# A fused RWKV and conv-gated MoE kernel: one planned rank per part of a chunk, per converted piece and per block of the feed-forward, with traced lengths in the planner and all of w_in on one DMA queue

## The chip, the cores and the metric

The kernel runs on one core of a Trainium2 chip. A core has five engines, each with its own instruction stream that is executed in order: PE (matrix multiply; its weight loads are shown as PEld), DVE, ACT, POOL and SP, which here only issues DMAs. The metric is the device time of one execution in microseconds. Before the change the median of three runs is 386.65 us (386.19 to 386.65).

## The reference, cut to what matters

```
for t in range(S):                      # B=4, H=8 heads, S=768, D=48
    y[t]  = r[t] @ (state + u * k[t] x v[t])
    state = w[t] * state + k[t] x v[t]
x = y as (B, S, 384)
h = relu(x @ w_in)                      # w_in 384 x 1024
conv = 3-tap convolution of h along S, one set of taps per hidden column
out = (h * sigmoid(conv)) @ w_out       # w_out 1024 x 384
```

w_in, conv_w and w_out arrive as 64-bit floats, and the kernel turns them into pairs of 32-bit values on the chip.

## The kernel before, in words

**Work.** The recurrence is cut into 24 chunks of 128 time steps (six per batch, numbered 0 to 23 here). Part A of a chunk transposes w, k and r on PE (L541), runs two scans on DVE (L548, L555), scales keys and receptances (L553, L559), makes the diagonal on POOL (L583, L585, L589) and transposes the keys back (L597). Part B makes the scores (L662), puts them under the diagonal (L666), updates the state (L679, L683), and sums the carried part (L718; L692 and L695 in the first four chunks) and the part within the chunk (L728; L702 and L707) into y. Two copies (L710 and L711, from chunk 4 on L733 and L735) write y to `xT` as two parts. Chunk loads of w, k, r and v are four DMAs of 192 KB (L509).

The feed-forward works on eight blocks of 384 time steps, two per batch. Block 0 needs the `xT` of chunks 0 to 3, block 1 that of chunks 2 to 5. A block has eight hidden tiles: nine matmuls each (L755, three for each third of the 384 inputs), then a chain on ACT, DVE and POOL (L767 to L777) that frees the tile's PSUM bank at L774 and makes `gh`. Its three output tiles take eight steps of three matmuls each (L784), are copied by ACT (L814) into one of two `val` buffers and stored by SP (L815).

**Weights.** w_in comes in three column pieces (384, 384, 256), each by four DMAs, two for partitions 0 to 63 and two for 64 to 127; SP issues the first pair and ACT the second (L479, L483). A piece is converted only when all four have landed, in three parts; w_out has eight parts (L494). Each part takes four DVE instructions (L439, L444, L447, L450), two casts on ACT (L442, L459) and two POOL instructions (L453, L460).

**Order.** Nothing is issued in the order of the code. `Plan.op` records each step with an engine, a length from the table `LEN`, what it reads and writes, and a rank; `Plan.issue` plays the program through: whenever an engine is free it takes the ready step of lowest rank for which buffers are free. The order that comes out is the instruction stream. Ranks before are formulas: chunk n has 14n (its loads 10 earlier, part B 7 later), hidden tile f of a block a base plus 5f, converted pieces 5 apart. DMAs use eight semaphores in turn, so an issue waits until the DMA eight issues earlier has landed, whichever queue that one was on.

Of the kernel before, what the change touches and what calls it, by code (L numbers as in the profile page):

```python
# [24 lines left out]
CHUNK, LEAD, UNIT, DOWN, PIECE = 14.0, 0.0, 5.0, 1.6, 5.0  # L25
FIRST_IN, FIRST_OUT = -10.0, 60.0
AHEAD, GUARD = 10.0, 10.0
# [8 lines left out]
    tr=0.35, kback=0.35, scores=1.1, carried=0.9, state=0.42, y=0.95, mm3=0.53,  # L36
    scan=0.86, small=0.1, pad=0.07, kt=0.47, dg=0.47, cp=0.62, xlo=0.6, sd=0.22, s=0.27,
    stt=0.54, gate=0.47, wts=0.47, wstt=0.47,
    fill=0.25, kh=0.42, guard=0.72, sbd=0.34, xhi=0.49, relu=0.5, mul=0.49, sig=0.43, cast=0.42, out=0.37, exp=0.52,
    z=0.98, diag=1.07, lo=0.97,  # L40
    gather=1.6, carried_rows=1.4, y_rows=1.5,
    load=0.55, issue=0.45, spread=0.64,
)
TAIL = dict(PE=0.22, DVE=0.11, ACT=0.13, POOL=0.07, SP=2.2)
# [66 lines left out]
class Plan:  # L111
# [6 lines left out]
    def op(self, eng, us, f, r=(), w=(), holds=(), moves=0.0, port=False, rank=None):  # L118
        i, deps = len(self.ops), set()
        us = LEN[us] if isinstance(us, str) else us  # L120
# [18 lines left out]
        self.ops.append((eng, us, f, deps, bufs, moves, port, (self.rank if rank is None else rank) + i * 1e-6))  # L139

    def issue(self):
        n = len(self.ops)
        left = [len(o[3]) for o in self.ops]
        users = [[] for _ in range(n)]
        for i, o in enumerate(self.ops):
            for d in o[3]:
                users[d].append(i)
# [5 lines left out]
        for i in range(n):  # L153
            if not left[i]:
                ready[self.ops[i][0]].append((self.ops[i][7], i))
        events, order, t = [], [], 0.0
# [17 lines left out]
        while len(order) < n:  # L174
            for e in engines:
                if free[e] > t:
                    continue
                for k, (_, i) in enumerate(sorted(ready[e])):
                    if places(self.ops[i][4]):
                        break  # L180
                else:
                    continue
                ready[e].remove((self.ops[i][7], i))
                _, us, _, _, _, moves, port, _ = self.ops[i]
                at = t
                if e == "PE" and t < COLD:
                    us *= 1.4
# [5 lines left out]
                free[e] = at + us  # L193
                if moves:
# [5 lines left out]
            assert t < float("inf"), "no order found"  # L200
# [5 lines left out]
            for i in todo:  # L206
                if i < 0:
                    continue
                for b in self.ops[i][4]:
# [4 lines left out]
                for u in users[i]:  # L214
                    left[u] -= 1
                    if not left[u]:
                        ready[self.ops[u][0]].append((self.ops[u][7], u))
        self.order = order
        for _, i in order:
            for b in self.ops[i][4]:  # L220
                if b.kind.make and not b.made:
                    b.t, b.made = b.kind.make(), True
            self.ops[i][2]()
# [72 lines left out]
def rwkv_conv_moe_kernel(  # L296
# [177 lines left out]
    def win_pieces(f0, n, piece, after):  # L474
# [3 lines left out]
        for g, (eng, q) in enumerate((("SP", nc.sync), ("ACT", nc.scalar))):  # L478
            op(eng, "issue", lambda g=g, q=q: q.dma_start(  # L479
                out=raw.t[64 * g:64 * g + D, :, 0:2 * n],  # L480
                in_=w_in[0:6 * D, cs].rearrange("(m g i) c -> g i m c", m=KT, g=2)[g]), [after] if g else [], [(raw, 2 * g)], [raw],
                moves=3.5 * n / 1024)
# [3 lines left out]
                moves=1.2 * n / 1024)  # L486
        for m in range(KT):
            plan.rank = next(piece)
# [3 lines left out]
    def wout_pieces(t0, n, piece):  # L492
# [3 lines left out]
            [], [(raw, 0)], [raw], moves=0.95 * n)  # L496
        for t in range(n):
            plan.rank = next(piece)
# [5 lines left out]
    def loads(n):  # L504
# [3 lines left out]
        for nm, src in (("w", w), ("k", k), ("r", r), ("v", v)):  # L508
            op("SP", "load", lambda nm=nm, src=src: nc.sync.dma_start(  # L509
                out=st[nm].t[:, :, 0:D], in_=src[b, :, s, :].rearrange("h t d -> t h d")), [], [st[nm]], moves=1.15)  # L510
# [15 lines left out]
    def stage_a(n):  # L526
# [7 lines left out]
        def tr(src, t, cols):  # L534
# [4 lines left out]
            def f():  # L539
                for m in range(KT):  # L540
# [4 lines left out]
        wp, kp, rp = Buf(pa), Buf(pa), Buf(pa)  # L545
        op("DVE", "pad", lambda: nc.vector.memset(wp.t[:, 0:WID:SL], 0.0), [], [(wp, 1)], [wp])
# [3 lines left out]
            op0=ALU.mult, op1=ALU.add), [wp, (wp, 1)], [kr])  # L550
        tr(K_, kp, lambda m: kp.t[:, m * L:(m + 1) * L])
        op("DVE", "small", lambda: nc.vector.reciprocal(out=da.t[:, 0:WID - 1:SL], in_=kr.t[:, 0, 1:WID:SL]), [kr], [da])
        op("DVE", "kt", lambda: nc.vector.tensor_tensor(out=seg(kr.t[:, 0], 2), in0=thirds(kp.t), in1=seg(kr.t[:, 0], 2),  # L553
                                                        op=ALU.mult), [kp], [kr])
        op("DVE", "scan", lambda: nc.vector.tensor_tensor_scan(  # L555
# [4 lines left out]
                                                        op=ALU.mult), [rp], [(kr, 1)], [kr])  # L560
        if n < EARLY:
# [11 lines left out]
        else:  # L573
            for g in range(2):
                for m in range(KT):
# [3 lines left out]
                        [last], moves=0.05)  # L579
        if n == 0:  # L580
# [13 lines left out]

        def k_back():
# [310 lines left out]
```

## Time and profile before

| | |
|---|---|
| median of 3 runs | 386.65 us |
| span of the profiled execution | 387.1 us |
| PE busy | 350.6 us, 91% of the span |
| DVE, ACT, POOL busy | 281.8, 234.5, 174.6 us |
| DMA | 34.46 MB |

The profiled execution's own time is given as its span, first to last instruction; it is 0.45 us above the median. An engine's busy time is the union of its instructions. The rows in the last section but one give busy time by stretches, timelines of single engines with the idle time before an instruction and who ended it, and the page's slices.

### The profile page before, as it was taken

The numbers are of one execution on the slowest core, as the hardware profiler recorded it, in microseconds if no ns is written. First come the engines' busy times: TensorE is split into PE (matmuls) and PEld (weight loads), VectorE is DVE, ScalarE is ACT, GpSimd is POOL, SyncE is SP. The second block draws the span as 40 slices with busy tenths as digits, with TensorE's granted clock in tenths as the row PEclk, the third lists the DMA queues.
The fourth block names the chain that finished last, engine by engine and source line by source line (L and its number), as shares of the span: only waits on it lengthen the run. The fifth ranks groups of instructions, "written<-read, shape, count | busy, mean of one in ns | idle before, by whom it ended". The sixth has DMA issues, their size and how long they took to land.

```text
span 387.1 us, 7859 instructions
## 1 busy us (share of the span) xinstructions
PE 350.6 (91%) x2790; PEld 320.3 (83%) x2790; DVE 281.8 (73%) x575; ACT 234.5 (61%) x613; POOL 174.6 (45%) x199
## 2 busy tenths in 40 slices
PE   5545978798899999999999999999999999999992
PEld 2435856687688999998999999999999989999992
DVE  4357989999998688578776876688867774656520
ACT  4133766687776565389747663697664725766621
POOL 5265596865785444056443532454544310434320
PEclk9856999899999999999999999999999999999998
DMA  9999984422334354373323447244424130110001
GB/s 150 151 159 179 231 242 98 92 53 49 66 66 99 69 107 78 89 153 85 73 60 75 88 96 143 56 102 94 93 52 94 41 75 10 30 33 20 22 20 69
DMA packets 113571, 34.46 MB, mean 89 GB/s; under 512 B 103069, under 2 KB 110774, under 8 KB 113526
## 3 DMA queue, kind: packets, MB, share of 16 engines
q1 hardware_dynamic: 112852, 32.32, 40.9%
q10 hardware_dynamic: 674, 1.57, 2.0%
q8 instruction: 24, 0.39, 0.4%
q14 instruction: 21, 0.17, 0.1%
HBM read 25.19 MB, written 4.72 MB: 77 GB/s over the span
## 4 chain that ended last, share of the span: by engine, by line
PE 71%; DVE 11%; DMA 5%; issue 3%; SPq 3%; ACT 3%; POOL 2%; ACTq 0%; DVEq 0%; POOLq 0%
PE bank L784 25%; PE bank L755 23%; PE bank L662 6%; PE bank L728 4%; PE bank L541 4%; PE bank L718 4%; PE bank L679 2%; SPq L509 2%; DMA v<-in_v_dram 2%; DMA gh<-in_moe_w_in_dram 2%; PE bank L597 2%; DVE pm L666 1%; DVE a L771 1%; DMA r<-in_r_dram 1%; DVE e L444 1%
## 5 line engine op out<-in xcount | busy, mean ns | idle before, releaser
L755 PE MATMUL bank<-xT,wi 128*128 128x386 f32 x576 | 129.0, 349 | 2.2 <-ACT xT L710 1.7
L784 PE MATMUL bank<-wo,gh 128*128 128x384 f32 x576 | 127.2, 344 | 2.1 <-POOL wo L460 1.7
L777 POOL TENSOR_TENSOR gh<-g,gh 128x384 fp32r<-128x384 f32 x64 | 64.7, 1015 | 114.5 <-ACT gh L776 109.6
L755 PEld LDWEIGHTS bank<-xT,wi 128*128 128x128 f32 x576 | 101.6, 190 | 5.7 <-issue 2.0
L784 PEld LDWEIGHTS bank<-wo,gh 128*128 128x128 f32 x576 | 100.2, 188 | 4.3 <-POOL wo L460 2.0
L769 DVE SCALAR_TENSOR_TENSOR a<-bank,cw,a 128x384 f32<-128x384 f32 x64 | 38.6, 609 | 23.1 <-ACT a L768 22.9
L774 DVE TENSOR_TENSOR g<-bank,a 128x384 f32<-128x384 f32 x64 | 34.8, 549 | 19.0 <-ACT a L773 18.2
L773 ACT ACTIVATE a<-a 128x384 f32<-128x384 f32 x64 | 33.4, 522 | 23.9 <-DVE a L771 23.8
L767 ACT ACTIVATE bank<-bank 128x386 f32<-128x386 f32 x64 | 30.6, 478 | 25.4 <-PE bank L755 24.5
L589 POOL TENSOR_SCALAR_AFFINE_SELECT pm<-dg 128x1024 f32<-128x1024 f32 x24 | 26.2, 1092 | 41.5 <-PE bank L728 39.1
L776 ACT CAST gh<-g 128x384 fp32r<-128x384 f32 x64 | 32.5, 512 | 12.2 <-DVE g L774 12.1
L771 DVE SCALAR_TENSOR_TENSOR a<-bank,cw,a 128x384 f32<-128x384 f32 x64 | 38.8, 611 | 0.8
L666 DVE COPY_PREDICATED pm<-upper,bank 128x512 f32<-128x512 int32 x48 | 33.5, 725 | 5.5 <-PE bank L662 5.2
L768 ACT ACTIVATE a<-bank,cw 128x384 f32<-128x384 f32 x64 | 36.7, 581 | 0.5
L583 POOL TENSOR_TENSOR z<-r,k 128x384 f32<-128x384 f32 x24 | 24.4, 1016 | 12.2 <-DMA r<-in_r_dram 12.2
L548 DVE TENSOR_TENSOR_SCAN kr<-bank,one_end 128x387 f32<-128x387 f32 x24 | 22.9, 956 | 9.2 <-PE bank L541 9.1
L453 POOL TENSOR_TENSOR val<-val,e 128x384 f32<-128x384 f32 (+2 forms) x18 | 16.7, 927 | 19.1 <-DVE val L450 8.0
L585 POOL TENSOR_TENSOR z<-z,ubc 128x384 f32<-128x384 f32 x24 | 24.2, 1008 | 1.2
L662 PEld LDWEIGHTS bank<-kr 48*128 48x128 f32 x288 | 18.4, 188 | 7.0 <-issue 4.1
L662 PE MATMUL bank<-kr 48*128 48x128 f32 x288 | 23.2, 290 | 0.9 <-DVE val L450 0.9
L555 DVE TENSOR_TENSOR_SCAN kr<-bank,dA 128x387 f32<-128x387 f32 x24 | 22.9, 953 | 0.1
L541 PE MATMUL bank<-ident,k 128*128 128x128 f32 x72 | 13.0, 293 | 10.6 <-ACT k L535 10.6
(108 smaller groups left out, 523.7 us busy)
## 6 DMA issues: line engine op xcount, KB each, us to landing
w<-in_w_dram SPq DMA_DIRECT2D x24, 192.0 KB, 3.1
k<-in_k_dram SPq DMA_DIRECT2D x24, 192.0 KB, 3.5
r<-in_r_dram SPq DMA_DIRECT2D x24, 192.0 KB, 3.6
v<-in_v_dram SPq DMA_DIRECT2D x24, 192.0 KB, 3.1
out_dram<-val SPq DMA_DIRECT2D x24, 192.0 KB, 2.0
gh<-in_moe_w_out_dram SPq DMA_DIRECT2D x2, 1152.0 KB, 8.4
last<-kr SPq DMA_DIRECT2D x120, 16.2 KB, 1.8
xT<-xT SPq DMA_DIRECT2D x18, 64.0 KB, 2.4
```

The lines of the kernel that those rows point to most:

```text
L662: nc.tensor.matmul(sc[g].t[:, m * L:(m + 1) * L], lhsT=kt(m)[p], rhs=rt(m)[p], start=True, stop=True)
L666: op("DVE", "cp", lambda g=g: nc.vector.copy_predicated(out=pm.t[:, g], mask=upper.unsqueeze(1).to_broadcast([P, NP, L]), data=sc[g].t.rea ...
L755: nc.tensor.matmul(t.t[:, 0:xs.stop - xs.start], lhsT=wi[:, m, a, f * P:(f + 1) * P], rhs=xT[:, x0 + m, c, xs], start=(m == 0 and j == 0), ...
L767: ("ACT", "relu", lambda: nc.scalar.activation(out=h(0, width + 2), in_=h(0, width + 2), func=AF.Relu), [t], [t]),
L768: ("ACT", "mul", lambda: nc.scalar.mul(out=a(), in_=h(1), mul=cw[:, 1, f:f + 1]), [t, "cw"], [a1]),
L769: ("DVE", "stt", lambda: nc.vector.scalar_tensor_tensor(out=a(), in0=h(0), scalar=cw[:, 0, f:f + 1], in1=a(), op0=ALU.mult, op1=ALU.add), ...
L771: ("DVE", "stt", lambda: nc.vector.scalar_tensor_tensor(out=a(), in0=h(2), scalar=cw[:, 2, f:f + 1], in1=a(), op0=ALU.mult, op1=ALU.add), ...
L773: ("ACT", "sig", lambda: nc.scalar.activation(out=a(), in_=a(), func=AF.Sigmoid), [], [a1]),
L774: ("DVE", "gate", lambda: nc.vector.tensor_tensor(out=g.t[:, 0:width], in0=h(1), in1=a(), op=ALU.mult), [t, a1], [g]),
L776: ("ACT", "cast", lambda: nc.scalar.copy(out=part(0)[:, 0:width], in_=g.t[:, 0:width]), [g], [key]),
L777: ("POOL", "lo", lambda: nc.gpsimd.tensor_tensor(out=part(1)[:, 0:width], in0=g.t[:, 0:width], in1=part(0)[:, 0:width].bitcast(F32), op=AL ...
L784: nc.tensor.matmul(acc.t[:, 0:DM], lhsT=part(a)[:, tt * P:(tt + 1) * P], rhs=wo[:, f, c, :], start=(f == 0 and a + c == 0), stop=(f == FT ...
```

## The change

The eight constants that made the ranks are gone. A table `RANKS` gives a rank for every chunk and each of its thirteen parts, for each of the 17 converted pieces, the nine weight loads, conv_w, the 64 hidden tiles and the 24 output tiles. The lengths in `LEN` are replaced by others. The planner now adds a length to a PE step when the way the array is tiled changes from the step before. Both halves of w_in are issued by SP, and all weight loads are recorded right after chunk 0's part A. The planner's search was rewritten with heaps. What is computed does not change.

```diff
-CHUNK, LEAD, UNIT, DOWN, PIECE = 14.0, 0.0, 5.0, 1.6, 5.0
-FIRST_IN, FIRST_OUT = -10.0, 60.0
-AHEAD, GUARD = 10.0, 10.0
+DOWN = 1.6
...
+RANKS = dict(
+    load=[-61.9, -47.0, 30.3, -29.9, 60.4, 81.8, -3.6, 26.6, 138.8, 36.5, 47.1, 52.2, 177.2, 85.5, 116.3, 144.5,
+        214.8, 252.8, 48.3, 184.5, 256.7, 194.0, 153.2, 286.8],
...
+SWITCH = {(FULL, ROW): 0.17, (TRANS, ROW): 0.17, (COL, ROW): 0.17, (FULL, COL): 0.11, (TRANS, COL): 0.11,
+          (FULL, TRANS): 0.08, (COL, TRANS): 0.05}
...
+    def at(self, part, i, more=0.0):
+        self.rank = RANKS[part][i] + more
...
+                if e == "PE":
+                    us = us * (1.4 if t < COLD else 1.0) + SWITCH.get((mode, m), 0.0)
+                    mode = m
...
-        for g, (eng, q) in enumerate((("SP", nc.sync), ("ACT", nc.scalar))):
+        for g, (eng, q) in enumerate((("SP", nc.sync), ("SP", nc.sync))):
+            plan.at("rows", 2 * (f0 // HB) + g)
...
-            plan.rank = base + f * UNIT
+            plan.at("hidden", FT * bi + f)
...
-                plan.rank = base + FT * UNIT + (f * 3 + tt if last else tt * FT + f) * DOWN
+                plan.at("out", 3 * bi + tt, (3 * f if last else f) * DOWN)
```

On SP, at the start of the program, before (the letter is the input, the digit before the underscore its buffer; `gh` holds a raw piece of w_in):

```order
L509 DMA w0_120<-in_w_dram 128x8x48
L509 DMA k0_122<-in_k_dram 128x8x48
L509 DMA r0_124<-in_r_dram 128x8x48
L509 DMA v0_126<-in_v_dram 128x8x48
L479 DMA gh_176<-in_moe_w_in_dram 48x3x768
L483 DMA gh_176<-in_moe_w_in_dram 16x3x768
L509 DMA w1_121<-in_w_dram 128x8x48
L509 DMA k1_123<-in_k_dram 128x8x48
L509 DMA r1_125<-in_r_dram 128x8x48
L509 DMA v1_127<-in_v_dram 128x8x48
```

And now, where the first piece of w_in comes with all four DMAs behind eight chunk loads:

```order
L592 DMA v0_126<-in_v_dram 128x8x48
L592 DMA w1_121<-in_w_dram 128x8x48
L592 DMA k1_123<-in_k_dram 128x8x48
L592 DMA r1_125<-in_r_dram 128x8x48
L592 DMA v1_127<-in_v_dram 128x8x48
L562 DMA gh_185<-in_moe_w_in_dram 48x3x768
L566 DMA gh_185<-in_moe_w_in_dram 16x3x768
L562 DMA gh_185<-in_moe_w_in_dram 48x3x768
L566 DMA gh_185<-in_moe_w_in_dram 16x3x768
L592 DMA w0_120<-in_w_dram 128x8x48
L592 DMA w1_121<-in_w_dram 128x8x48
```

Chunk 1's loads moved ahead of the first piece, and the loads of chunks 2 and 3 follow it in pairs.

On ACT, around the fill of chunk 1's k (`k1`), before:

```order
L535 COPY w1_121<-w1_121 128x2x3x16
L605 ACTIVATE junk_75,flags_112<-w1_121,guard_hi_110 128x384
L442 ACTIVATE bank2_66<-bank2_66,ebias_118 128x384
L459 CAST wi_116<-val0_72 128x384
L479 DMA gh_179<-in_moe_w_in_dram 48x3x768
L535 COPY k1_123<-k1_123 128x2x3x16
L535 COPY r1_125<-r1_125 128x2x3x16
```

and now:

```order
L618 COPY w1_121<-w1_121 128x2x3x16
L698 ACTIVATE junk_75,flags_112<-w1_121,guard_hi_110 128x384
L698 ACTIVATE junk_75,flags_112<-w1_121,guard_lo_108 128x384
L618 COPY k1_123<-k1_123 128x2x3x16
L618 COPY r1_125<-r1_125 128x2x3x16
```

The DMA issue that stood ahead of `k1` on ACT is gone, and no conversion stands between them.

On PE, at the first hidden tile (`xT` times `wi`) and the scores of chunk 4 (from `kr1`), before:

```order
L755 MATMUL bank4_68<-xT_113,wi_116 128x386 x9
L662 MATMUL bank6_70<-kr1_134 128x128
...
L728 MATMUL bank6_70<-pm0_154,v1_127 48x128 x8
L755 MATMUL bank2_66<-xT_113,wi_116 128x386 x3
```

and now:

```order
L855 MATMUL bank1_65<-xT_113,wi_116 128x386 x3
L855 MATMUL bank3_67<-xT_113,wi_116 128x386 x3
L855 MATMUL bank1_65<-xT_113,wi_116 128x386 x3
L855 MATMUL bank3_67<-xT_113,wi_116 128x386 x3
L855 MATMUL bank1_65<-xT_113,wi_116 128x386 x3
L855 MATMUL bank3_67<-xT_113,wi_116 128x386 x3
L855 MATMUL bank4_68<-xT_113,wi_116 128x386 x3
L757 MATMUL bank6_70<-kr1_134 128x128
```

Two hidden tiles and a third of the next stand ahead of chunk 4's scores, where one stood.

## Rows read from the trace of the kernel before

**Rows 1.** The page: busy time and share of each engine, and the span in 40 slices (tenths of busy time).

```profile
PE 350.6 (91%) x2790; PEld 320.3 (83%) x2790; DVE 281.8 (73%) x575; ACT 234.5 (61%) x613; POOL 174.6 (45%) x199
PE   5545978798899999999999999999999999999992
```

**Rows 2.** Busy time by stretches: us, then busy us of each engine with its instructions, the granted clock, the DMA engines' share, GB/s.

```profile
0.00:57.00 57.00, 36.17 (x293) 28.80 (x293) 36.94 (x88) 26.02 (x82) 31.96 (x57) 0.82 1.01 181
57.00:70.00 13.00, 8.64 (x96) 7.08 (x94) 12.99 (x29) 9.02 (x28) 8.20 (x10) 1.00 0.45 111
70.00:114.00 44.00, 40.02 (x301) 34.60 (x302) 43.23 (x89) 33.17 (x85) 31.36 (x33) 0.96 0.34 69
114.00:380.00 266.00, 265.63 (x2106) 249.78 (x2105) 188.46 (x370) 165.82 (x418) 103.08 (x102) 1.00 0.33 71
```

**Rows 3.** The timeline of ACT at the fills of k for chunks 1 and 2: start, length, what, and in brackets the idle time before it and who ended it. ACTq is a DMA issue.

```profile
20.64 0.51 ACT L459 CAST wi<-val 128x384 fp32r<-128x384 f32 x1
25.63 0.32 ACTq L479 DMA_DIRECT2D gh<-in_moe_w_in_dram  x1
25.99 0.27 ACT L535 COPY k<-k 128x96 f32<-128x96 f32 x1 [4.83 <-DMA gh<-in_moe_w_in_dram]
...
34.70 0.27 ACT L535 COPY k<-k 128x96 f32<-128x96 f32 x1 [3.07 <-DMA v<-in_v_dram]
```

**Rows 4.** The timeline of PE at the same two places.

```profile
26.31 0.90 PE L541 MATMUL bank<-ident,k 128*128 128x128 f32 x3 [5.43 <-ACT k L535]
...
35.02 0.90 PE L541 MATMUL bank<-ident,k 128*128 128x128 f32 x3 [3.40 <-ACT k L535]
```

**Rows 5.** Who DVE waited for in the first 57 us: total us, times, longest.

```profile
DVE bank L439 <- DMA gh<-in_moe_w_in_dram: 5.6, 1, 5.6
DVE e L444 <- ACT bank L442: 5.2, 2, 4.3
DVE kr L548 <- PE bank L541: 2.9, 1, 2.9
```

**Rows 6.** Busy time of two early stretches of 10 us, columns as in rows 2.

```profile
10.00:20.00 10.00, 5.45 (x50) 4.82 (x48) 3.75 (x9) 2.41 (x9) 2.64 (x4) 0.79 1.06 152
...
30.00:40.00 10.00, 5.67 (x32) 4.96 (x30) 7.64 (x15) 4.54 (x16) 6.07 (x6) 0.66 1.15 178
```

**Rows 7.** The timeline of DVE: the first conversion, and a stretch without idle time.

```profile
17.39 0.56 DVE L439 TENSOR_SCALAR bank<-gh 128x384 int32<-128x384 int32 x1 [5.57 <-DMA gh<-in_moe_w_in_dram]
...
89.10 0.61 DVE L771 SCALAR_TENSOR_TENSOR a<-bank,cw,a 128x384 f32<-128x384 f32 x1
89.62 0.73 DVE L666 COPY_PREDICATED pm<-upper,bank 128x512 f32<-128x512 int32 x1
90.24 0.54 DVE L450 SCALAR_TENSOR_TENSOR val<-gh,bank 128x384 f32<-128x384 uint32 x1
90.70 0.55 DVE L774 TENSOR_TENSOR g<-bank,a 128x384 f32<-128x384 f32 x1
```

**Rows 8.** The timeline of PE, at the first hidden tile and at the eighth output step.

```profile
69.94 0.45 PE L755 MATMUL bank<-xT,wi 128*128 128x386 f32 x1 [1.67 <-ACT xT L710]
70.69 2.94 PE L755 MATMUL bank<-xT,wi 128*128 128x386 f32 x8 [0.30 <-DVE xT L711]
...
90.92 1.08 PE L728 MATMUL bank<-pm,v 128*48 128x128 f32 x16
91.93 0.80 PE L755 MATMUL bank<-xT,wi 128*128 128x386 f32 x3
...
112.38 1.22 PE L784 MATMUL bank<-wo,gh 128*128 128x384 f32 x6
```

**Rows 9.** The timeline of PE in the stretch without idle time.

```profile
203.30 0.49 PE L597 MATMUL bank<-ident,kr 128*128 128x128 f32 x3
203.54 0.78 PE L755 MATMUL bank<-xT,wi 128*128 128x386 f32 x3
204.16 0.69 PE L784 MATMUL bank<-wo,gh 128*128 128x384 f32 x3
204.69 0.69 PE L755 MATMUL bank<-xT,wi 128*128 128x386 f32 x3
...
210.59 0.94 PE L662 MATMUL bank<-kr 48*128 48x128 f32 x12
...
211.68 0.67 PE L679 MATMUL bank<-v,kh 128*64 128x48 f32 x16
212.28 0.91 PE L718 MATMUL bank<-kr,sbd 112*112 112x128 f32 x6
...
213.25 0.49 PE L541 MATMUL bank<-ident,w 128*128 128x128 f32 x3
213.58 0.49 PE L541 MATMUL bank<-ident,k 128*128 128x128 f32 x3
```

**Rows 10.** The timeline of ACT at the end of the program.

```profile
378.99 1.00 ACT L814 COPY val<-bank 128x384 f32<-128x384 f32 x2 [6.71 <-PE bank L784]
381.45 0.48 ACT L814 COPY val<-bank 128x384 f32<-128x384 f32 x1 [1.47 <-DMA out_dram<-val]
```

**Rows 11.** The page's DMA issues: KB each and us from issue to landing.

```profile
last<-kr SPq DMA_DIRECT2D x120, 16.2 KB, 1.8
```

**Rows 12.** The timeline of SP, where it issues the six small DMAs of a chunk (`last`).

```profile
66.28 3.94 SPq L576 DMA_DIRECT2D last<-kr  x6
```

More of the change, by code (lines that the diff above doesn't have):

```diff
@@ L35 @@
 LEN = dict(
[L36 to L40, printed above, removed]
+    tr=0.3, kback=0.3, scores=0.93, carried=0.8, state=0.6, y=1.0, mm3=0.53,
+    scan=0.875, small=0.1, pad=0.07, kt=0.465, dg=0.44, cp=0.62, xlo=0.6, sd=0.3, s=0.265,
+    stt=0.527, gate=0.465, wts=0.461, wstt=0.461,
+    fill=0.172, kh=0.335, guard=0.61, sbd=0.364, xhi=0.483, relu=0.41, mul=0.475, sig=0.426, cast=0.418, out=0.375,
+    exp=0.48, z=0.97, diag=1.06, lo=0.966,
     gather=1.6, carried_rows=1.4, y_rows=1.5,
@@ L44 @@
+FULL, TRANS, ROW, COL = range(4)
+MODE = dict(tr=TRANS, kback=TRANS, gather=TRANS, carried=TRANS, carried_rows=TRANS, scores=ROW,
+            state=COL, y=COL, y_rows=COL)
+SWITCH = {(FULL, ROW): 0.17, (TRANS, ROW): 0.17, (COL, ROW): 0.17, (FULL, COL): 0.11, (TRANS, COL): 0.11,
+          (FULL, TRANS): 0.08, (COL, TRANS): 0.05}
 TAIL = dict(PE=0.22, DVE=0.11, ACT=0.13, POOL=0.07, SP=2.2)
@@ L138, in op, with reset, run @@
                     t.kind.wanted += 1
[L139 to L147, printed above, removed]
+        self.ops.append((eng, us, f, deps, bufs, moves, port, self.rank + i * 1e-6, mode))
+    def reset(self):
+        kinds, stores = {}, {}
+        for o in self.ops:
+            for x in o[4]:
+                kinds[id(x.kind)] = x.kind
+        for k in kinds.values():
+            k.held = k.served = k.wanted = 0
+            stores[id(k.places)] = k
+        for k in stores.values():
+            if not hasattr(k, "all"):
+                k.all = list(k.places)
+            k.places[:] = k.all
+        seen = set()
+        for o in self.ops:
+            for x in o[4]:
+                if id(x) not in seen:
+                    seen.add(id(x))
+                    x.t, x.uses, x.turn = None, 0, x.kind.wanted
+                    x.kind.wanted += 1
+                x.uses += 1
+    def run(self, ranks):
+        self.reset()
+        ops, n = self.ops, len(self.ops)
+        left = [len(o[3]) for o in ops]
         engines = ("PE", "DVE", "ACT", "POOL", "SP")
@@ L154, in issue @@
             if not left[i]:
-                ready[self.ops[i][0]].append((self.ops[i][7], i))
-        events, order, t = [], [], 0.0
+                heapq.heappush(ready[ops[i][0]], (ranks[i], i))
+        events, order, t, end, mode = [], [], 0.0, 0.0, FULL
         def places(bufs):
@@ L193, in issue @@
                 free[e] = at + us
+                end = max(end, free[e])
                 if moves:
@@ L213, in issue @@
                         b.kind.places.append(b.t)
-                for u in users[i]:
+                for u in self.users[i]:
                     left[u] -= 1
                     if not left[u]:
-                        ready[self.ops[u][0]].append((self.ops[u][7], u))
+                        heapq.heappush(ready[ops[u][0]], (ranks[u], u))
+        return order, end
+    def issue(self):
+        ops, n = self.ops, len(self.ops)
+        self.users = [[] for _ in range(n)]
+        for i, o in enumerate(ops):
+            for d in o[3]:
+                self.users[d].append(i)
+        ranks = [o[7] for o in ops]
+        order, end = self.run(ranks)
         self.order = order
         for _, i in order:
-            for b in self.ops[i][4]:
+            for b in ops[i][4]:
                 if b.kind.make and not b.made:
                     b.t, b.made = b.kind.make(), True
-            self.ops[i][2]()
+            ops[i][2]()
 def general(ctx, tc, r, k, v, w, u, out, const, ident, x, moe_block):
```

126 lines of the change are left out of this document (87 added, 39 removed), and 4 rows, old and new, of the table hidden.

## The prediction

> **What bounds the kernel now.** I read the page first. PE is busy for 91% of the span, DVE for 73%; the slices show that PE's missing share lies at the start and in the last slice, where everything between is 9 [rows 1]. Then I cut the span where the character changes [rows 2]. From 114 to 380 us PE is busy 265.6 of 266 us: nothing but less work for PE shortens that. From 70 to 114 us it is DVE that is full (43.2 of 44), and PE loses 4.0 us in small waits. From 57 to 70 us DVE is full as well (13.0 of 13), PE has 8.6. From 0 to 57 us neither is: PE has 36.2, DVE 36.9, and the DMA engines are busy throughout (share 1.01). So PE's idle time is 20.8 + 4.4 + 4.0 + 0.4 = 29.6 us, and behind it a tail of 7 us. Anything that a new order gains has to come out of these 29.6, by bringing DVE through its early work sooner, or out of the tail.
>
> Who made DVE wait early: the first conversion for w_in's first piece (5.6 us), an instruction behind ACT (4.3), and the start (2.9) [rows 5]. The 4.3 and two waits of PE have one origin. ACT had finished a cast at 21.15 and then stood before a DMA issue until 25.63, because that issue waits for an earlier DMA to land; the fill of k for chunk 1 was queued behind it. The same happened before the fill at 34.70, with 3.07 us [rows 3]. PE, which needs the filled k, waited 5.43 and 3.40 us there [rows 4].
>
> **The change, step by step.** *Lengths, SWITCH, heaps, RANKS* cost nothing themselves: they act in the planner, and what counts is the order.
>
> *w_in by SP.* Six issues leave ACT, at 0.32 us each [rows 3] some 1.9 us, and with them the two waits of 4.8 and 3.1 us. SP gets six issues more. It has nothing else to do, and its DMA engines were the limit anyway: 152 to 178 GB/s in the early stretches at a share of 1.06 to 1.15 [rows 6]. The bytes are the same, so I take no DMA time gained or lost; from outside, half of ACT's waits could come back as later landings (4 us), or the shared engines gain a little (1 us). The Trainium skill, "DMA: Bandwidth & Descriptors", section "Issuing engines are not separate DMA queues", says that DMAs started by several engines share the same 16 DMA engines, and that starting them on several saves only the sequencer's issue time. By that rule alone the two halves on one queue would return the 1.9 us of issue time to ACT, and the forecast would be some 5 us higher; the trace shows more than issue time, the 7.9 us for which ACT was held ahead of its fills.
>
> *When data arrives.* The first piece of w_in now stands behind eight loads: 8 x 192 + 1152 KB = 2.75 MB. Before, 2.16 MB had gone when the piece was there at 17.3 us [rows 7]; 0.59 MB more at 0.152 MB/us is 3.9 us: 21.2 us. The loads of chunks 2 and 3 (1.57 MB at 0.16) are then in at 31 us. The second piece, with half of the third and conv_w mixed in (1.6 MB at 0.178), is complete at 40.
>
> *DVE until the first hidden tile.* Both orders need the xT of chunks 0 to 3. Before, the fourth copy released PE at 70.69 us [rows 8]; DVE had been busy for 49.9 of the first 70 [rows 2], so it had idled for 20. Counted along DVE, exactly twelve instructions fewer now stand ahead of it, all of conversions, 0.46 us apart (90.24 to 90.70) [rows 7]: 5.5 us less, 45 us of work. Idle time now: the start 3.9 us (to the first scan, as before); chunks 0 and 1 keep DVE fed to about 17.5 (11.5 us of work to the first xT copy, some waits), then up to 4 us for the piece at 21.2; from there work runs to 40, where the second piece arrives, say 1 us; 3 to 4 us for small waits on PE and ACT. Sum 12.5 us; bounds 8 (the piece costs nothing) and 20 (all idle time returns elsewhere). The fourth xT copy is then done at 57.5, and PE's first hidden tile starts at 58.5 instead of 69.94 [rows 8]. PE's own work ahead of it, 44.8 us by then [rows 2], fits.
>
> *From there to block 1.* In the new order PE does, from the first hidden tile of block 0 to that of block 1, 24 thirds and 20 output steps at 0.53 us, three scores at 1.09, two states at 0.60, two carried at 0.97, seven transposes at 0.33, two back at 0.24 [rows 9], three y at 1.01 [rows 8]: 23.3 + 12.2 = 35.5. A step after another tiling takes 0.62 in place of 0.53 (203.54 to 204.16) [rows 9]; 15 such returns add 1.4: 36.9. DVE in the same stretch, up to the xT copy of chunk 5: 27 conversion instructions at 0.46, 24 of hidden tiles at 0.52 (89.10 to 89.62) [rows 7], and 25 of attention: 12.4 + 12.6 + 11.3 = 36.3. The two are level, so I charge the waits that PE has when DVE is full: 4.0 per 44 us [rows 2], here 3.5. Block 1 starts at 58.5 + 36.9 + 3.5 = 98.9 us.
>
> *The same work before.* At 112.38 us [rows 8] PE had done 33 thirds and 7 output steps, and of attention the same but for one transpose group and one back more. Four steps less those two are 1.55 us: before was there at 113.9. So 15.0 us are won at this point.
>
> *Given back.* DVE stays near full until the conversions are through, at about 135 us; at the same rate 3.5 us go there. I count 228 changes of tiling along PE against 220 before, at 0.09 us: 0.7 us.
>
> *The tail.* Before, the last block's three output tiles end together. ACT copies two at 378.99 and the third waits 1.47 us, to 381.45, for a store to release its buffer [rows 10]. Now one of the three ends eight steps (4.2 us) early, and the last finds a free buffer: 1.3 us won.
>
> Sum: 387.1 - 15.0 + 3.5 + 0.7 - 1.3 = 375.0 us of span. The profiled execution's span stands 0.45 us above the median; the forecast of the median is 374.6 us.
>
> **Rivals.**
> 1. *The early idle time stays.* DVE waits for w_in as long as before in sum, 20 us: each piece needs all four DMAs, and with 64 partitions of it behind loads and behind another piece's halves the last quarter can be late. For it: the DMA share above 1 [rows 6]. Against it: the waits of rows 3 are tied to an issue that is gone. Then the first tile starts at 66 instead of 58.5; 7.5 us less gain: 382.1.
> 2. *A late wait takes it back.* The new order packs chunks 20 to 23 tightly ahead of the last two blocks: from the y of chunk 19 to that of chunk 23 PE finds only eleven output steps between the chunks. Each chunk needs six small DMAs through SP (3.94 us to issue) [rows 12], the last landing 1.8 us later [rows 11], into one of two buffers that is free only after the carried part two chunks back. I count 6.4 us of PE work between release and need for chunk 21, against 5.7 to 6 for the DMAs: room of half a us. If other issues on SP stand ahead of them, each of the four chunks becomes a chain: DMAs 5.7, scores 1.1, masking two times 0.62 (89.62 to 90.24) [rows 7], y 1.0, about 9 us where PE has about 5 of work, 16 us in all: 390.6, slower. It decides when the DMAs start 3 us late in each round; for it, SP's strict order; against it, that PE lost 0.4 us in 266 with the same DMAs in looser order [rows 2].
> 3. *The order changes nothing that counts*: gains early, but PE, short of ready hidden tiles later, loses as much: 386. PE's full stretch speaks against it.
> 4. *More is won*: DVE idles for only 8 us early and the waits of 3.5 twice do not occur: 375 - 4.5 - 5 = 365.5 at most.
>
> **How the numbers follow.** The forecast (370 to 380) has 0.55, rival 1 (380 to 385.8) 0.20, rival 2 0.13, rival 3 0.05, rival 4 (below 370) 0.07. A measurement of this kernel can tell about 0.2% from no change, that is 385.9 to 387.4. Faster by more than that: 0.55 + 0.20 + 0.07 = 0.82. Within it: 0.05. Slower: 0.13. The range from 368 to 386 leaves out rival 2, the lower part of rival 4 and half of rival 3: just under 0.2.
>
> **What would show it.** In the changed profile: no DMA issue on ACT before a fill of k, and PE's waits of 5.4 and 3.4 us gone; the first hidden tile at 56 to 61 us; DVE idle 11 to 14 us before it; PE through block 1's first hidden tile by 99; at most 4 us of idle PE from there to 135 and 1 us after; the last copy on ACT without a wait for a store. A first hidden tile after 64 would show rival 1, idle PE above 5 us after 250 rival 2, and idle time spread over 135 to 370 would show rival 3.

## The result and the profile after

The changed kernel takes 373.65 us (median of 4 runs, 373.06 to 375.82) against 386.65: a ratio of 0.967, 95% interval 0.964 to 0.970. The forecast was 374.6.

The traced execution of the changed kernel has a span of 371.4 us. First the page, which answers to [rows 1], with the slices of the granted clock:

```profile
PE 347.4 (94%) x2790; PEld 317.2 (85%) x2790; DVE 281.7 (76%) x575; ACT 233.9 (63%) x613; POOL 174.5 (47%) x199
PE   7967776999999999999999999999999999999992
PEclk9999996999999999999999999999999999999998
```

And its stretches, the columns as in [rows 2]:

```profile
0.00:57.00 57.00, 43.96 (x402) 35.10 (x402) 47.93 (x113) 33.74 (x108) 38.48 (x64) 1.00 0.94 193
57.00:70.00 13.00, 10.91 (x72) 9.71 (x74) 12.14 (x26) 10.91 (x28) 9.95 (x10) 0.74 0.34 93
70.00:114.00 44.00, 42.67 (x335) 38.25 (x332) 40.64 (x86) 30.73 (x81) 27.80 (x28) 1.00 0.42 90
114.00:364.00 250.00, 249.61 (x1985) 234.03 (x1983) 180.83 (x352) 157.92 (x396) 98.27 (x97) 1.00 0.32 71
```

Most of what changed is in the first row. DVE does 47.9 us of work in the first 57 us instead of 36.9, PE 44.0 instead of 36.2. PE's idle time in the four stretches was 20.8, 4.4, 4.0 and 0.4 us before; it is 13.0, 2.1, 1.3 and 0.4 now. Behind 114 us PE is full in both kernels. Every span here splits into three parts: PE's idle time up to its last instruction, its busy time, and the tail behind it. Before: 29.5 + 350.6 + 7.0 = 387.1. After: 16.9 + 347.4 + 7.1 = 371.4. So 12.6 us of idle time went, and 3.2 us of busy time, though PE executes the same 2790 instructions. The busy time goes with the clock: before, the granted clock was at half (1.2 instead of 2.4 GHz) from 15.9 to 29.5, from 32.9 to 39.8 and from 70.5 to 73.9 us; after, only from 58.8 to 65.7. PE was busy for 13.1 us of the first three stretches and 5.0 of the last; if half of that is the price of the clock (an estimate), it is 6.5 against 2.5 us. The page's slices of the granted clock before, to set beside those above:

```profile
PEclk9856999899999999999999999999999999999998
```

The fills of k for chunks 1 and 2 on ACT, where [rows 3] have waits of 4.83 and 3.07 us behind a DMA issue:

```profile
8.78 0.19 ACT L698 ACTIVATION_READ_ACCUMULATOR junk<-w,guard_lo 128x1 f32 x1
8.87 0.25 ACT L618 COPY k<-k 128x96 f32<-128x96 f32 x1
...
21.03 0.54 ACT L524 ACTIVATE bank<-bank,ebias 128x384 int32<-128x384 int32 x1
21.49 0.26 ACT L618 COPY k<-k 128x96 f32<-128x96 f32 x1
```

No wait and no DMA issue is left there, and chunk 1's k is filled at 8.87 us instead of 25.99. PE's timeline, to be read beside [rows 4], [rows 8] and [rows 9]: the transposes of k for chunks 1 and 2, the first hidden tile, what follows it, the first step of block 1, and the only wait behind 114 us:

```profile
11.39 0.49 PE L624 MATMUL bank<-ident,k 128*128 128x128 f32 x3
...
21.80 0.55 PE L624 MATMUL bank<-ident,k 128*128 128x128 f32 x3 [0.88 <-ACT k L618]
...
51.44 0.44 PE L855 MATMUL bank<-xT,wi 128*128 128x386 f32 x1 [0.43 <-ACT xT L809]
...
57.24 0.82 PE L757 MATMUL bank<-kr 48*128 48x128 f32 x9 [0.98 <-DVE e L526]
...
62.06 4.18 PE L855 MATMUL bank<-xT,wi 128*128 128x386 f32 x13 [1.85 <-DVE val L532]
...
97.76 0.78 PE L855 MATMUL bank<-xT,wi 128*128 128x386 f32 x3
...
281.42 0.55 PE L689 MATMUL bank<-ident,kr 128*128 128x128 f32 x3 [0.39 <-DVE kr L640]
```

Of the waits of 5.43 and 3.40 us the first is gone and the second is 0.88. The first hidden tile starts at 51.44 instead of 69.94, block 1 at 97.76. DVE's first conversion, which stood idle for 5.6 us before [rows 5]:

```profile
18.21 0.56 DVE L521 TENSOR_SCALAR bank<-gh 128x384 int32<-128x384 int32 x1 [1.05 <-DMA gh<-in_moe_w_in_dram]
```

The piece of w_in itself comes no earlier (18.21 against 17.39). What changed is how much other work stands ahead of it on DVE.

### The profile page after: what moved, and what is told of

It is laid out like the page before. It is cut to its first block, busy times and chain, and to the rows that moved or that the text cites. A ratio compares the mean times of both kernels' runs of the same rounds, so it can differ in the third digit from the quotient of the medians.

```text
span 371.4 us, 7867 instructions
## 1 busy us (share of the span) xinstructions
PE 347.4 (94%) x2790; PEld 317.2 (85%) x2790; DVE 281.7 (76%) x575; ACT 233.9 (63%) x613; POOL 174.5 (47%) x199
## 4 chain that ended last, share of the span: by engine, by line
PE 71%; DVE 15%; DMA 3%; ACT 3%; issue 3%; SPq 3%; POOL 1%; DVEq 0%; ACTq 0%
PE bank L855 26%; PE bank L884 24%; PE bank L827 5%; PE bank L757 5%; PE bank L817 4%; PE bank L624 4%; DMA gh<-in_moe_w_in_dram 2%; PE bank L776 2%; SPq L592 2%; DVE kr L632 2%; PE bank L689 1%; DVE val L532 1%; DVE pm L762 1%; DVE kr L643 1%; DVE a L869 1%
## 5 line engine op out<-in xcount | busy, mean ns | idle before, releaser
L855 PE MATMUL bank<-xT,wi 128*128 128x386 f32 x576 | 123.3, 350 | 2.4 <-DVE val L532 1.8
L884 PE MATMUL bank<-wo,gh 128*128 128x384 f32 x576 | 122.8, 344 | 1.2 <-POOL wo L542 1.0
L884 PEld LDWEIGHTS bank<-wo,gh 128*128 128x128 f32 x576 | 99.2, 188 | 4.1 <-POOL wo L542 1.7
L869 DVE SCALAR_TENSOR_TENSOR a<-bank,cw,a 128x384 f32<-128x384 f32 x64 | 38.2, 612 | 26.3 <-ACT a L868 26.0
L873 ACT ACTIVATE a<-a 128x384 f32<-128x384 f32 x64 | 33.4, 524 | 20.7 <-DVE a L871 20.2
L867 ACT ACTIVATE bank<-bank 128x386 f32<-128x386 f32 x64 | 29.8, 473 | 21.4 <-PE bank L855 20.6
L871 DVE SCALAR_TENSOR_TENSOR a<-bank,cw,a 128x384 f32<-128x384 f32 x64 | 38.3, 610 | 1.3 <-DVE a L869 0.6
L876 ACT CAST gh<-g 128x384 fp32r<-128x384 f32 x64 | 31.8, 511 | 10.2 <-DVE g L874 7.7
L673 POOL TENSOR_TENSOR z<-r,k 128x384 f32<-128x384 f32 x24 | 24.4, 1017 | 28.7 <-DMA r<-in_r_dram 13.1
L868 ACT ACTIVATE a<-bank,cw 128x384 f32<-128x384 f32 x64 | 35.8, 578 | 1.2 <-DVE g L874 0.6
L757 PE MATMUL bank<-kr 48*128 48x128 f32 x288 | 24.0, 290 | 1.0 <-DVE e L526 1.0
L749 ACT COPY sbd<-sd 48x192 f32<-48x192 f32 x34 | 11.9, 349 | 19.7 <-DVE sd L736 19.5
```

Source lines behind the costliest of these rows:

```text
L757: nc.tensor.matmul(sc[g].t[:, m * L:(m + 1) * L], lhsT=kt(m)[p], rhs=rt(m)[p], start=True, stop=True)
L855: nc.tensor.matmul(t.t[:, 0:xs.stop - xs.start], lhsT=wi[:, m, a, f * P:(f + 1) * P], rhs=xT[:, x0 + m, c, xs], start=(m == 0 and j == 0), ...
L868: ("ACT", "mul", lambda: nc.scalar.mul(out=a(), in_=h(1), mul=cw[:, 1, f:f + 1]), [t, "cw"], [a1]),
L869: ("DVE", "stt", lambda: nc.vector.scalar_tensor_tensor(out=a(), in0=h(0), scalar=cw[:, 0, f:f + 1], in1=a(), op0=ALU.mult, op1=ALU.add), ...
L871: ("DVE", "stt", lambda: nc.vector.scalar_tensor_tensor(out=a(), in0=h(2), scalar=cw[:, 2, f:f + 1], in1=a(), op0=ALU.mult, op1=ALU.add), ...
L873: ("ACT", "sig", lambda: nc.scalar.activation(out=a(), in_=a(), func=AF.Sigmoid), [], [a1]),
```

## The experiments

Three questions: is it the queue or the order, which part of the order, and what does the clock do. Idle, busy and tail are as above; "half" is the time at half clock up to PE's last instruction, and behind it PE's busy time in it; all from the one traced execution of each kernel. Ratios are to the kernel before on the same chip, whose median there was 386.65 to 387.70 us.

| kernel | median us | ratio, 95% interval | first hidden tile | idle | busy | tail | half (busy in it) |
|---|---|---|---|---|---|---|---|
| before | 386.65 | 1 | 69.9 | 29.5 | 350.6 | 7.0 | 23.9 (13.1) |
| changed | 373.65 | 0.967 (0.964 to 0.970) | 51.4 | 16.9 | 347.4 | 7.1 | 6.8 (5.0) |
| e1_queue_only | 386.93 | 1.001 (0.998 to 1.005) | 67.2 | 23.7 | 354.3 | 6.8 | 23.9 (20.0) |
| e2_act_queue | 405.56 | 1.048 (1.042 to 1.053) | 65.7 | 34.2 | 362.3 | 7.6 | 30.7 (28.1) |
| e3_new_early | 378.03 | 0.978 (0.973 to 0.982) | 52.4 | 21.1 | 347.8 | 6.2 | 3.4 (3.3) |
| e4_new_late | 407.06 | 1.053 (1.048 to 1.058) | 63.2 | 32.1 | 362.9 | 7.6 | 30.7 (26.1) |
| e5_old_order_sp | 384.92 | 0.995 (0.993 to 0.997) | 65.1 | 24.3 | 352.8 | 6.7 | 23.9 (19.1) |
| e6_new_order_act | 375.63 | 0.972 (0.967 to 0.978) | 56.1 | 20.2 | 347.2 | 6.9 | 3.4 (3.4) |
| e7_old_lengths | 389.75 | 1.007 (1.002 to 1.011) | 48.9 | 21.5 | 358.6 | 7.1 | 23.8 (22.0) |
| e8_new_lengths | 384.61 | 0.995 (0.992 to 0.998) | 63.9 | 22.3 | 353.0 | 6.8 | 20.4 (16.5) |
| e9_tail_together | 374.08 | 0.968 (0.964 to 0.973) | 51.6 | 14.8 | 349.3 | 7.6 | 10.2 (9.9) |
| e10_clock_before | 388.61 | 1.004 (1.002 to 1.006) | 67.5 | 20.3 | 357.7 | 7.0 | 6.8 (6.8) |
| e11_clock_after | 373.60 | 0.967 (0.963 to 0.970) | 52.4 | 14.0 | 350.5 | 7.0 | 3.4 (3.4) |
| e12_more_search | 375.26 | 0.969 (0.965 to 0.973) | 53.5 | 16.5 | 350.5 | 7.2 | 13.7 (11.5) |

### The queue, with the planner free to order anew

e1_queue_only, the kernel before with:

```diff
-        for g, (eng, q) in enumerate((("SP", nc.sync), ("ACT", nc.scalar))):
+        for g, (eng, q) in enumerate((("SP", nc.sync), ("SP", nc.sync))):
...
-  [after] if g else [], [(raw, 2 * g)], [raw],
+  [], [(raw, 2 * g)], [raw],
```

> The kernel before, with both halves of each piece of w_in issued by SP and nothing else of the change. Theory A (ACT's DMA issues, which held the fills of k, made the early idle time): the waits of PE of 5.43 and 3.40 us go, the first hidden tile starts about 8 us earlier than 69.94, at 60 to 64, and the time is 379 to 382. Theory B (what counts is the order of the loads and of the early work, not who issues them): SP's queue only shifts the waits, the first hidden tile stays at 67 to 71 and the time at 385 to 388.

e2_act_queue, the changed kernel with:

```diff
-        for g, (eng, q) in enumerate((("SP", nc.sync), ("SP", nc.sync))):
+        for g, (eng, q) in enumerate((("SP", nc.sync), ("ACT", nc.scalar))):
```

> The changed kernel, with the second half of each piece of w_in issued by ACT as before. Theory A: ACT stands before its DMA issues again, the first hidden tile falls from 51.4 back to 56 to 60, and the time rises by 5 to 8 us, to 379 to 382. Theory B: ACT's issues find their places in the new order without holding anything that PE needs, the first hidden tile stays at 51 to 53, and the time rises by at most 2 us, to 373.5 to 376.

e1 is at 386.93, no change, in theory B's range. e2 is at 405.56, 32 us above the changed kernel and far outside what either theory allowed. One entry of one line had changed, but the planner takes that entry into its model and made another order from it, from chunk 1's first transposes on. So neither run says what the queue is worth. The next two hold the order.

### The queue, with the order held

e5_old_order_sp plans the second half as ACT's and issues it by SP; e6_new_order_act plans it as SP's and issues it by ACT. All other instructions stand as in the kernel that each is made from.

```diff
-        for g, (eng, q) in enumerate((("SP", nc.sync), ("ACT", nc.scalar))):
+        for g, (eng, q) in enumerate((("SP", nc.sync), ("ACT", nc.sync))):
```

> The kernel before with its whole order held, instruction for instruction, on PE, DVE, ACT and POOL; only ACT's six DMAs for w_in are issued by SP, at the same places of the planned order. Theory A (ACT's waits in front of the fills of k are lost time): PE's waits of 5.43 and 3.40 us go or fall under 1.5, the first hidden tile comes at 62 to 66 and the time at 379 to 384. Theory B (DVE and PE wait for bytes, whoever issues them): the waits return in front of other instructions, the first hidden tile at 69 to 71, the time at 385.5 to 388.

```diff
-        for g, (eng, q) in enumerate((("SP", nc.sync), ("SP", nc.sync))):
+        for g, (eng, q) in enumerate((("SP", nc.sync), ("SP", nc.scalar))):
```

> The changed kernel with its whole order held on PE, DVE, ACT and POOL; the second half of each piece of w_in is issued by ACT instead of SP, at the same places of the planned order. Theory A: ACT stands at these issues, each of which waits for the DMA eight issues earlier to land, the fills behind it are late, the first hidden tile moves from 51.4 to 55 or later, the time to 377 to 382. Theory B: less than 1.5 us, 373 to 375. In either case far from the 405.6 us of the version that the planner ordered anew, if that one's loss lies in its order and not in the queue.

e5 wins 0.5% or 1.9 us, clear of noise. e6 loses 2.0 against the changed kernel's median, but its interval overlaps the changed kernel's. Both times lie between the ranges of the two theories. Where the 8 us of ACT's waits went, PE and DVE of e5 show:

```profile
20.65 1.09 PE L679 MATMUL bank<-v,kh 128*64 128x48 f32 x16 [6.53 <-ACT kh L599]
21.68 0.90 PE L541 MATMUL bank<-ident,w 128*128 128x128 f32 x3
23.07 0.90 PE L541 MATMUL bank<-ident,k 128*128 128x128 f32 x3 [0.49 <-ACT k L535]
```

```profile
19.08 0.56 DVE L439 TENSOR_SCALAR bank<-gh 128x384 int32<-128x384 int32 x1 [7.77 <-DMA gh<-in_moe_w_in_dram]
```

The wait for k is 0.49 us instead of 5.43, and one of 6.53 stands just ahead of it. In the old order the first conversion comes early in DVE's row and waits 7.77 us for w_in; ACT's part of that conversion stands ahead of the copy of `kh` that PE needs. So the wait was not ACT's issue alone.

e6's first hidden tile comes 4.7 us late, but not in theory A's way: no wait of ACT up to there stands behind one of its issues of w_in. Two of these now go out at 3.75 and 4.46 us, where on SP they stood behind chunk 1's loads (8.42 and 8.88). Chunk 1's w, issued by SP at 3.56 us as in the changed kernel (3.57), lands at 12.1 instead of 7.3. ACT and PE of e6, and PE of the changed kernel:

```profile
12.13 0.27 ACT L618 COPY w<-w 128x96 f32<-128x96 f32 x1 [3.43 <-DMA w<-in_w_dram]
...
12.45 0.90 PE L624 MATMUL bank<-ident,w 128*128 128x128 f32 x3 [5.51 <-ACT w L618]
```

```profile
7.67 0.90 PE L624 MATMUL bank<-ident,w 128*128 128x128 f32 x3 [0.79 <-ACT w L618]
```

All that follows is late by this. In the new order the queue acts through which bytes land first; of the 4.7 us some 2 are left at the end.

### The parts of the order

e3_new_early and e4_new_late choose a rank by whether the part belongs to the beginning; `old_rank` returns the formulas of the kernel before.

```diff
-        self.rank = RANKS[part][i] + more
+        self.rank = (RANKS[part][i] if early_part(part, i) else old_rank(part, i)) + more
```

> The changed kernel, with the new ranks only for chunks 0 to 7, w_in's pieces and rows, conv_w and block 0; the old formulas for all later chunks and blocks. Theory A (the whole gain is made before block 1): first hidden tile at 51 to 53, time within 2 us of the changed kernel, 372 to 376. Theory C (the ranks of the later chunks keep PE fed after 100 us, and without them a part of the gain is given back): first hidden tile as early, but 4 us or more of idle PE behind 100 us, time 377 to 383.

> The opposite: the old formulas for chunks 0 to 7, the pieces and block 0, the new ranks for all that is later; both halves of w_in by SP as in the changed kernel. Theory A (the gain is made before block 1 by the order): first hidden tile at 62 to 70, time 381 to 387. Theory C (later ranks carry a part of the gain): the time falls below 380 though the first hidden tile is as late as that.

e3 keeps 8.6 of the 13 us: its first hidden tile is as early (52.4) and its clock as good. The rest is idle time that the later ranks had avoided. Two of its stretches, the first number behind the comma PE's busy time:

```profile
114.00:200.00 86.00, 84.96 (x727) 78.23 (x727) 69.19 (x137) 59.39 (x155) 40.32 (x40) 1.00 0.43 91
200.00:300.00 100.00, 98.95 (x818) 91.22 (x814) 76.20 (x150) 62.02 (x163) 41.69 (x41) 1.00 0.37 80
```

That is theory C. Against the changed kernel PE idles 1.7 us more behind 114 us (2.1 against 0.4), 1.7 more from 57 to 114, and 2.0 just before its last instruction, where the flag's step waits for ACT's last copy (the tail behind it is 0.9 us shorter for it); in the first 57 us it idles 1.1 us less. e4 lies above both ranges, 20 us slower than before: in this mix new ranks for late parts are worse than none. That they count on the early beginning which belongs to them is likely, but not shown.

e7_old_lengths puts the old `LEN` back and counts no tiling changes; e8_new_lengths uses `old_rank` for every part and keeps the rest of the change.

```diff
-                    us = us * (1.4 if t < COLD else 1.0) + SWITCH.get((mode, m), 0.0)
+                    us = us * (1.4 if t < COLD else 1.0) + 0.0
```

> The changed kernel with the table of lengths of before and tiling changes counted as nothing in the planner; ranks and queue as changed. If the ranks carry the gain: within 3 us of the changed kernel, 373 to 377. If ranks and lengths only work as a pair (the ranks are numbers that fit one run of the planner): PE waits in many small places, 382 to 405.

```diff
-        self.rank = RANKS[part][i] + more
+        self.rank = old_rank(part, i) + more
```

> The changed kernel with the rank formulas of before for every part; the new lengths, the tiling changes and the one queue stay. If lengths and queue carry the gain: 373 to 379. If the ranks carry it: first hidden tile at 64 to 70 and a time of 383 to 390.

Neither half carries the gain: e7 lies in the range of ranks and lengths that work only as a pair, e8 in that of ranks that carry it. With the new lengths and the old formulas the time is 384.61, about what the queue alone brought in e5; with the new ranks and the old lengths 389.75, slower than before. e7 also shows that the first hidden tile alone proves little: it starts at 48.9, earlier than in the changed kernel, but PE reaches block 1 only at 115.2. Its stretches:

```profile
57.00:70.00 13.00, 11.88 (x101) 10.62 (x100) 11.34 (x24) 11.55 (x30) 6.15 (x7) 0.99 0.37 96
70.00:114.00 44.00, 36.46 (x270) 30.24 (x270) 42.02 (x89) 27.04 (x74) 35.04 (x36) 0.88 0.34 69
114.00:380.00 266.00, 262.03 (x2029) 242.24 (x2025) 183.97 (x360) 166.25 (x411) 98.82 (x98) 1.00 0.31 69
```

DVE is nearly full from 70 to 114 us (42.0 of 44) and PE starves there (36.5), as in [rows 2].

Both kernels keep two edits that the section on the change does not name: the planner's amounts for DMAs (`moves`, for w_in's issues 7.0 and 3.6 instead of 3.5 and 1.2, for w_out 1.05 instead of 0.95, for a chunk load 1.05 instead of 1.15), and the second half of a piece no longer depends on a chunk's w. With the ranks of before they bring nothing beyond e8's 2 us. A search for ranks with the old lengths was not run, so what the traced lengths are worth to a search stays open.

### The tail

```diff
+                if last:
+                    plan.rank = 420.0 + (3 * f + tt) * DOWN
```

> The changed kernel, with the last block's three output tiles ending together as in the kernel before; the order is otherwise the same almost to the last instructions. By the forecast's term for the tail (the third copy waits for a store to give its buffer back) the time rises by 1.3 us, to 375. By the other reading (the end is set by SP's load of the flag and the branch behind it, not by a store) it stays within 0.7 us, 373.0 to 374.4.

374.08: 0.4 us up, within what the runs can tell. The wait for the store is back in e9; ACT's last copy:

```profile
365.44 0.48 ACT L916 COPY val<-bank 128x384 f32<-128x384 f32 x1 [1.44 <-DMA out_dram<-val]
```

and SP's load of the flag and its branch behind it (name, count, ns, start in us), in e9:

```profile
L970 SPq TENSOR_LOAD <-inside x1: 483/483/483, 364.4 to 364.4; - x1
...
L971 SPq COMPARE_BRANCH  x1: 45/45/45, 366.3 to 366.3; - x1
```

in the changed kernel, with PE's branch:

```profile
L968 SPq TENSOR_LOAD <-inside x1: 489/489/489, 365.1 to 365.1; - x1
...
L969 PEldq COMPARE_BRANCH  x1: 3673/3673/3673, 365.1 to 365.1; - x1
...
L969 SPq COMPARE_BRANCH  x1: 45/45/45, 366.0 to 366.0; - x1
```

In e9 (and before) SP loads the flag while the third copy waits for its buffer, and branches right after the last store's issue. In the changed kernel that issue is 1.2 us earlier (364.7 against 365.9), but the load, 0.9 us with what belongs to it, now stands behind it. SP's branch moves by 0.35 us, from 366.34 to 365.98, and the end of the span with it, from 371.70 to 371.35. Counted from PE's last instruction, SP's branch comes after 2.24 us before, 2.26 in e9 and 1.74 in the changed kernel: of the 1.3 us 0.5 are there. From the branch to the end of the span it is 4.76 us before, but 5.37 in the other two traces, and these 0.6 us hide the 0.5 (tails of 7.0, 7.6 and 7.1). A part is that SP goes on 2.87 us after its branch in the trace of before, and 3.16 in the others. What holds it there, PE's branch of 3.7 to 4.0 us among others, is left open.

### The clock

e10 and e11 keep the order and add 128x128 transposes of the identity into banks that the next instruction overwrites, in PE's waits; they add work and leave none out.

```diff
+                for _ in range(HOLD.get(at, 0)):
+                    self.nc.tensor.transpose(out=b.t[:, 0:128], in_=self.still, identity=self.still)
```

> The kernel before with its order held on every engine, and 87 additional 128x128 transposes of the identity, each into a bank that the next instruction overwrites, put into seven of PE's long early waits (up to 35 us), to keep PE active there. If PE's idle waits are what brings the clock to half, the granted clock stays 1.00 up to 40 us (before: half for 20.5 us up to there), PE's busy time without the additions falls by some 5 us; the time falls by 1 to 4 us, since a part of that lay beside waits anyway. If the clock falls for another reason, it stays at half from 15.9 to 29.5 and from 32.9 to 39.8, and the time rises by 0 to 4 us for the additions.

> The changed kernel with its order held and 39 such additional transposes in nine of PE's waits between 7 and 51 us. If PE's idle waits bring the clock down, the half-clock stretch from 58.8 to 65.7 us goes or moves and the time falls by up to 2.5 us, to 371 to 373.5. If not, the stretch stays and the time is 373.5 to 376.

e10's stretches, with the granted clock in the third column from the right:

```profile
15.90:29.50 13.60, 9.91 (x93) 8.75 (x92) 8.34 (x18) 6.20 (x19) 5.89 (x7) 0.87 1.12 179
29.50:40.00 10.50, 7.22 (x81) 6.57 (x80) 8.91 (x21) 5.02 (x19) 7.03 (x7) 1.00 1.18 213
40.00:57.00 17.00, 13.42 (x142) 11.15 (x141) 16.22 (x39) 12.10 (x40) 13.02 (x15) 1.00 0.91 241
57.00:70.00 13.00, 10.03 (x102) 8.16 (x102) 13.00 (x31) 7.79 (x24) 8.14 (x9) 1.00 0.29 59
```

With PE's waits filled, the clock up to 40 us is at half for 3.4 us instead of 20.5: it was PE's idling ahead of it that had brought it down. The first hidden tile comes 2.4 us sooner (67.5). Yet the time rises, by 0.2 to 0.6%. So a clock held there wins nothing that would outweigh the additions; what these cost where they outlast a wait, the runs don't separate. In e11 the half-clock time falls from 6.8 to 3.4 us, and the time stays. Its stretch speaks for DVE as what limits it there:

```profile
58.80:65.70 6.90, 4.49 (x17) 4.16 (x17) 6.90 (x15) 6.20 (x17) 6.42 (x8) 0.76 0.40 130
```

DVE is busy for 6.90 of 6.90 us there, PE for 4.49 at a clock of 0.76, after 5.05 at 0.51 in the changed kernel.

### A further search

e12_more_search is the changed kernel with another table of ranks, found by carrying the search for numbers on, on the planner itself.

```diff
-    load=[-61.9, -47.0, 30.3, -29.9, 60.4, 81.8, -3.6, 26.6, 138.8, 36.5, 47.1, 52.2, 177.2, 85.5, 116.3, 144.5,
...
+    load=[-1352.1, -1041.9, -520.0, -908.2, 442.2, 833.6, -551.8, -2102.0,
...
```

> The changed kernel with other numbers in RANKS: the same search for ranks carried further on the planner with the same lengths. If an order that the planner with the traced lengths prefers is better on the chip too, 370 to 372.5. If the gain of the last few us in the planner is below what its lengths can tell (it knows nothing of the clock), 373 to 377.

375.26 (0.969) against the changed kernel's 0.967: not better. PE's idle time is as short as the change's (16.5), but the half-clock time is twice as long, and PE's busy time 3.1 us higher:

```profile
0.00:57.00 57.00, 46.11 (x396) 37.84 (x397) 47.05 (x111) 32.70 (x105) 35.82 (x61) 0.91 0.97 196
57.00:114.00 57.00, 52.30 (x382) 46.05 (x380) 51.16 (x107) 42.04 (x109) 40.48 (x41) 0.97 0.40 83
114.00:364.00 250.00, 249.09 (x1996) 233.46 (x1997) 182.30 (x357) 156.72 (x398) 98.73 (x97) 1.00 0.33 72
```

No run here is measurably faster than the changed kernel.

## Why the prediction was right, and where not

The direction and the place were right: DVE is brought through its early work sooner, some 12 us of PE's idle time go, and nothing is lost late. That the number came out within 1 us is in part luck: two errors of 7.1 and 5.9 us on the way to block 1 nearly cancel, and so, in part, do an error of 3.6 us in the span and one of 2.7 us in the step from span to median. By its steps:

*ACT's two waits.* They went as foretold, but the forecast gave them too much weight: it set "the 7.9 us for which ACT was held ahead of its fills" against the price of issuing alone, 1.9 us. With the order held, the queue is worth some 2 us (e5, e6), and the gain lies in the order. The number is close to what the rule of the Trainium skill gave, which the forecast had weighed and put aside ("DMA: Bandwidth & Descriptors", section "Issuing engines are not separate DMA queues": issuing from several engines saves only issue time). That it is issue time is not shown: in e6 no issue holds ACT, and the loss starts with chunk 1's w, which lands 4.8 us later. So "no DMA time gained or lost" was wrong too: the bytes are the same, but the queue changed when they land.

*The first piece at 21.2 us, the first hidden tile at 58.5.* Mis-sized: 18.2 and 51.4, the latter outside the sign that the forecast gave (56 to 61). The 0.59 MB more ahead of the piece were charged with 3.9 us, and it came 0.8 us later than before: the DMA engines moved 172 and 178 GB/s in the first two stretches of 10 us, 149 and 152 before. Why they did is open. DVE's idle time ahead of the first hidden tile is 7.6 us, where the forecast took 12.5 and gave 8 as its lower bound. The new order gives DVE work of chunks 0 and 1 until the piece is there (a wait of 1.05 us) and keeps it nearly full from 20 to 50 us.

*Block 1 by 98.9.* 97.8, but by two errors that cancel. Of the 7.1 us by which the first tile was early 1.1 were left, because the stretch from there to block 1 took 46.3 us where the forecast had 40.4:

```profile
51.44:97.76 46.32, 42.01 (x303) 36.69 (x304) 43.77 (x92) 33.96 (x89) 36.18 (x38) 0.93 0.38 84
```

PE does there what the forecast counted, group by group. It is idle for 4.3 us instead of 3.5, with waits of 0.98 and 1.85 us for DVE, but busy for 42.0 instead of 36.9. Half of the 5.0 us at half clock, 2.5, is an estimate of one part of these 5.1; the rest stays open. DVE is busy for 43.8 of the 46.3 us, in 92 instructions where the forecast had 76 and 36.3 us. So DVE is nearly full, and a lead of PE may just wait for it, but no run tests that. For the same work, before took until 113.9 by the forecast's count; so 16.1 us were won there instead of 15.0.

*3.5 us given back, and 0.7 for tiling changes.* The first did not come: behind block 1 PE waits once, 0.39 us. From block 1 to the end the changed kernel takes 371.4 - 97.8 = 273.6 us, before from 113.9 on 273.2. So of the forecast's 2.9 us net behind block 1, 0.4 came. The 3.5 us are the largest error among the four terms of the sum.

*The tail, 1.3 us won.* Failed: the tail is 7.1 us instead of 7.0, though the last copy does find a free buffer. The term counted the copy's wait alone; SP's load of the flag had lain inside that wait and now stands behind the last issue. Measured against e9, 0.5 of the 1.3 us are there, and 0.6 us behind SP's branch, of open cause, take them back.

*The clock.* The forecast took no account of it. PE's busy time fell by 3.2 us at the same instructions. e10 and e11 speak against a term of its own: a clock held up by filling the waits gave nothing. What a clock that stays up without added work is worth, no run shows.

*From span to median.* The forecast set the traced span of before, 387.1, beside the median of 386.65. But a run's time is some 1.7 to 2.0 us above its span: runs of before that are listed with both have 387.99 for 386.0 and 384.67 for 382.7. So the traced execution of before was about 2.4 us longer than the median one. The spans fell by 15.7 us, where the forecast had 12.1; the medians fell by 13.0, where it had 12.05. So these two errors largely cancel, which is luck: the sum of the span came out 3.6 us too high (375.0 for 371.4), the step to the median 2.7 us too low (0.45 below the span, where the changed kernel's median is 2.25 above).

*The rivals.* The early idle time did not stay (rival 1). The dense chunks 20 to 23 did no harm (rival 2): the one wait near them is the 0.39 us at 281.4. What was underrated is how brittle such an order is: e2, e4 and e7, each with a part of the change taken back, are at 390 to 407 us, where the forecast's worst rival was 390.6. Idle and half-clock time account for most of it. By the table, with half of the busy time at half clock taken off, PE's work is 343 to 346 us in the other kernels without additions, but 348 to 350 in these three; what these 3 to 5 us are stays open.

## What to carry to other kernels

In a kernel whose order a planner makes, an edit that the planner sees is two edits, its own effect and a new order; hold the order and try the edit alone before giving it a price (2 us here, where the free planner made 0 and 32 of it). Ranks found by search fit one table of lengths and one another: a part of them kept 8.6 of the 13 us (e3), another was worth less than none (e4). And a wait that is removed is worth only what the next instruction does not wait for: look, in the old order, at what stands right behind it.

## What the runs showed of the hardware

- A DMA issue can wait for an earlier DMA whatever its data. In the trace of before 299 DMAs use eight semaphores, 37 or 38 times each, in turn, and an issue that takes one has to wait until that one's last DMA has landed, also where the other queue had issued it. ACT's issue at 25.63 us waits for the semaphore of SP's issue of w_in at 17.52, the one at 34.34 for that of SP's load of v at 25.85. That is what held ACT for 4.83 and 3.07 us [rows 3].
- A DMA that a second engine issues takes its share of the DMA engines from those already under way: with w_in's issues at 3.75 and 4.46 us on ACT, a load issued by SP at 3.56 landed at 12.1 us instead of 7.3 (e6 against the changed kernel).
- The branch behind the flag, taken by every engine, takes PE 3.7 to 4.0 us and ACT, POOL and SP 0.05 (three traces: before, changed, e9).
- The clock fell where PE had idled and came back while it was busy; filling PE's waits with transposes held it (up to 40 us, half for 3.4 us instead of 20.5), without making the kernel faster.
